# Block 2's keys and queries turned by TensorE inside block 1's units

## The chip, the cores and the metric

The kernel runs on one core of one Trainium2 chip. The metric is the device time of one execution in microseconds (us); lower is better. Before the change the median of 7 runs is 243.35 us (242.52 to 245.54).

## What is computed

Chunked attention with a few memory keys, and then a gated feed-forward layer on its output. Inputs and the output are float32.

```python
# q, k, v: (4, 8, 768, 64); mem_k, mem_v: (4, 8, 8, 64)
for c in range(24):                               # chunks of 32 queries
    l_start, r_end = max(0, 32*c - 16), min(768, 32*c + 32 + 8)
    k_full = concat([mem_k, k[:, :, l_start:r_end]], axis=2)
    v_full = concat([mem_v, v[:, :, l_start:r_end]], axis=2)
    scores = q[:, :, 32*c:32*c + 32] @ k_full.T / 8
    out[:, :, 32*c:32*c + 32] = softmax(scores) @ v_full
x = out.transpose(0, 2, 1, 3).reshape(3072, 512)
y = (maximum(x @ w_gate, 0) * (x @ w_val)) @ w_out    # 512 -> 1536 -> 512
```

## The kernel before

The 3072 rows of x are cut into 8 blocks of 384 tokens (half a sequence each; `TB`, `NB`). For each block the attention is done for four pairs of heads (`hp` 0 to 3). A block has four groups of 96 queries (three chunks each), and each group sees 8 memory rows and a band of 120 keys, so its scores are a 128 x 96 tile with the keys on the partitions. For scores on TensorE (PE), keys and queries must stand with the head's 64 numbers on the partitions, while in memory they stand by token. The step that brings them there is called a turn here.

There are two kinds of turn. Blocks 0 and 1 load keys and queries in long rows, four tokens (1 KB in float32) to a row (`load_rows`), and TensorE turns them: `turn_pe` issues 8 small matmuls against a 0/1 matrix `sels` that also picks the overlapping windows of the keys, and 8 against the identity for the queries. VectorE (DVE) copies the result from PSUM to `kq` (`turn_copy`): for block 0 in one copy of 896 columns, for block 1 in two of 512 and 384. Blocks 2 to 7 load bands and tokens, one token (256 bytes) to a row (`load_band`, `load_q_tokens`), and `turn_dma` turns them with two DMA transposes that SyncE (SP) issues. From block 4 on, GpSimd (POOL) then copies the queries to a tile with zeros between the two heads of a pair (`spread_q`, `qbds`), with which four wide matmuls make the scores of a pair in place of eight narrow ones (`step_s`).

After the scores ScalarE (ACT) takes the exponential. Blocks 0 and 1 get the sums by a matmul with ones (`wide_d`), their inverse by ScalarE (`wide_e`) and the weighted values by `wide_v`. Later blocks hold ones beside the values in `vwins`, so that one matmul gives values and sums (`step_v`), then come the inverse (`step_e`) and the multiply by VectorE (`step_m`). The 0/1 words of `vwins` are written by `one_words`, memsets on VectorE.

The feed-forward part of a block is 12 units and 3 output units. A unit (`ffn_unit`) is 4 matmuls for the gate and 4 for the value, a ReLU by ScalarE (`gr`) and a product by VectorE (`gv`, L343). An output unit (`out_unit`) is 12 matmuls, a copy by ScalarE, and the store.

The order of the instructions on each engine is written out by hand, and each engine runs its own in that order. Block 0's attention comes first, then block 0's units 2 to 11 with block 1's attention between them. Then `run` walks a list of units and places the four steps of the next block's attention: the scores of pair `hp` after unit `at[hp]`, values and inverse `wait` units later, the multiply one unit after that. The first `run` goes over block 1's twelve units and then the six output units of blocks 0 and 1, with block 2's attention at units 11, 12, 14 and 15. Each later `run` goes over one block's units with the next block's attention.

GpSimd issues all loads from HBM that convert float32 to float16, one after the other; a load waits until the eighth before it has landed. The weights of the units come in column groups (`load_w`): 0 to 256, 256 to 512, 512 to 768, 768 to 1024 and 1024 to 1536. Block 1's rows are loaded after the third of these. PSUM has one tile of two banks for scores (`sps`, tag sc), one bank each for `xo` and `xs`, and four banks for units (`fps`); block 0's turns use two tiles of their own before those four exist.

Of the kernel before, what the change touches and what calls it, by code (L numbers as in the profile page):

```python
# [17 lines left out]
def kernel(  # L18
# [158 lines left out]
    def turn_pe(n, hp):  # L177

        if n == 0:
            ps = pools["t"].tile([128, 2, 512], F32, tag="t", name="kq_ps")  # L180
            kps, qps = ps[:, 0], ps[:, 1, 0:TB]
        else:
            ps, kps, qps = None, bank("k_ps"), bank("q_ps")[:, 0:TB]
        turns[n, hp] = ps, kps, qps
        rk, rq = (t.rearrange("p h (j d) -> p h j d", j=J) for t in rows_of(n))
        sel = sels[n].rearrange("p i t -> p (i t)")
        for j in range(J):
# [10 lines left out]
    def turn_copy(n, hp):  # L198
# [5 lines left out]
        ps, kps, qps = turns.pop((n, hp))  # L204
        if n == 0:
            dve_copy(turns[n][:, hp], ps.rearrange("p a c -> p (a c)")[:, 0:512 + TB])
        else:
            dve_copy(turns[n][:, hp, 0:512], kps)
            dve_copy(turns[n][:, hp, 512:], qps)
# [40 lines left out]
    def step_s(n, hp):  # L250
        sc = sps.tile([128, 2, 512], F32, tag="sc", name="sc_ps")
        view = sc[:, :, 0:TB].rearrange("p a (c m) -> p a c m", m=QB)
        if n < 4:
            score_mms(n, hp, sc, True)
# [120 lines left out]
    def fill(count):  # L375
        for i in range(count):
            nc.tensor.matmul(xo, lhsT=filler[:, 0:128], rhs=filler[:, 0:TB], start=True, stop=True)
# [58 lines left out]
    fetch_mem(memk, mem_k)  # L436
    for c0 in (0, 256, 512):
        load_w(c0, c0 + 256)

# [16 lines left out]
    with tc.tile_pool(name="tps", bufs=2, space=bass.MemoryType.PSUM) as pools["t"]:  # L456
# [9 lines left out]
        turn_copy(0, 1)  # L466
        turn_pe(0, 2)
        turn_copy(0, 2)
        wide_d(0, 0)
        wide_e(0, 0)  # L470
        step_s0(0, 1)
        turn_pe(0, 3)
        turn_copy(0, 3)
    pools["f"] = ctx.enter_context(tc.tile_pool(name="fps", bufs=4, space=bass.MemoryType.PSUM))
    step_s0(0, 2)
    wide_d(0, 1)
    wide_e(0, 1)
    fill(2)
    step_s0(0, 3)
    fill(1)  # L480
    wide_v(0, 0)
# [10 lines left out]
    select(bias, 0.0, -NMEM, [[0, 3]], 1, ALU.is_ge)  # L492
    select(bias, NEG, NMEM + 55, [[32, 3]], -1, ALU.is_ge)
    load_w(768, 1024)

# [13 lines left out]
    load_mem_v(1)  # L509
    load_w(1024, 1536)  # L510

    ffn_unit(0, 2, spare=True)
    zero(words(k16s[0][0:32, 0].rearrange("p h d -> p (h d)")), 0)
    zero(words(k16s[1][96:128, NQ - 1].rearrange("p h d -> p (h d)")), 0)
    load_mem_k(2)
    load_mem_k(3)
    load_band(2, k, k16s)
    load_q_tokens(2)
    turn_dma(2)
    wo_src = moe_w_out.rearrange("(c p) f -> p c f", p=128)  # L520
    for a in range(0, NDC, 4):
        pool_dma(wo[:, a:a + 4, :], wo_src[:, a:a + 4, :])

    def value(n, hp):
        wide_v(n, hp)

# [3 lines left out]

    for m in range(3, 6):
        ffn_unit(0, m)
    one_words(0, 0, 128, 0, NQ, ONE)
    one_words(0, 0, NMEM + 16, 0, 1, 0)
    one_words(0, 0, NMEM, 0, 1, ONE)
    load_band(2, v, vwins)
    load_mem_v(2)
    turn_pe(1, 0)
# [4 lines left out]
    turn_pe(1, 2)  # L543
    turn_copy(1, 2)
    step_s(1, 1)
    turn_pe(1, 3)
    turn_copy(1, 3)
    ffn_unit(0, 6)
    sums(1, 0)
    step_s(1, 2)  # L550
    ffn_unit(0, 7)
    sums(1, 1)
    step_s(1, 3)
    value(1, 0)
    ffn_unit(0, 8)
    value(1, 1)
    sums(1, 2)
    ffn_unit(0, 9)
    value(1, 2)
    sums(1, 3)  # L560
    ffn_unit(0, 10)
    value(1, 3)
    ffn_unit(0, 11)


# [16 lines left out]

    def run(order, n, at, wait, turn_at):
        for u, (b, x) in enumerate(order):
            if n < NB:
                pieces(n, [("m", hp) for hp in range(HP) if u == at[hp] + wait + 1])
                now = [hp for hp in range(HP) if u == at[hp] + wait]
                inner, outer = ("ve", "") if x >= NDC else ("v", "e")
                unit(b, x, [lambda w=(w, hp): pieces(n, [w]) for hp in now for w in inner])
                pieces(n, [(w, hp) for hp in now for w in outer])  # L590
                pieces(n, [("s", hp) for hp in range(HP) if u == at[hp]])
            else:
                unit(b, x)
            if u == turn_at and n + 1 < NB:
                turn_dma(n + 1)
                if n + 1 > 3:
                    spread_q(n + 1)
            if n == 2 and u < len(clear):
                clear[u]()

    def loads(n):
        if n < NB:
            load_band(n, k, k16s)
            if n > 3:
                load_mem_k(n)
            load_q_tokens(n)
            load_band(n, v, vwins)
            load_mem_v(n)

    loads(3)  # L610
    run([(1, m) for m in range(NDC)] + [(b, NDC + t) for b in range(2) for t in range(NT)],
        2, (11, 12, 14, 15), 2, 13)
    pieces(2, [("m", 3)])
    for n in range(2, NB):
        loads(n + 2)
        run([(n, u) for u in range(NDC + NT)], n + 1, (3, 6, 8, 11) if n == 2 else (0, 3, 6, 9), 2, 9)

# [29 lines left out]
```

## Time and profile before

| | before |
|---|---|
| median of 7 runs | 243.35 us |
| time given for the profiled execution | 243.35 us |
| its span in the profile | 241.4 us |
| mean granted TensorE clock | 0.992 |
| TensorE (PE) busy | 228.2 us (95%), 1691 matmuls |
| ScalarE (ACT) busy | 144.0 us (60%) |
| VectorE (DVE) busy | 101.3 us (42%) |
| GpSimd (POOL) busy | 99.3 us (41%) |
| DMA queue of GpSimd | 86896 packets, 15.17 MB |
| DMA queue of SyncE | 24922 packets, 6.43 MB |

The profile is one execution as the hardware profiler recorded it. Its span runs from the program's first instruction to its last, and the time of a run has some more around it. Busy time is a union of instruction times, so an engine that is busy for 95% may still not be at its peak. "Granted clock" is the share of full speed that TensorE was given. A line such as `PE L336 MATMUL g_ps<-xT,wg` names the engine, the line of the kernel, the operation, and the tiles that it writes and reads; an arrow in brackets names what ended the idle time before it.

### The profile page before, as it was taken

The page shows a single profiled execution, that of the slowest core. Times are in us where ns is not written, and L with a number is a line of the kernel's source. Part 1 is how long each engine was busy: PE and PEld are TensorE (multiplying, and loading weights), DVE is VectorE, ACT ScalarE, POOL GpSimd, SP SyncE. Part 2 cuts the span into 40 slices and gives each one's busy share as a digit, 9 for nine tenths or more (in the row PEclk, how much of TensorE's full clock was granted, in tenths as well). Part 3 has the DMA queues.
Part 4 walks back from the last instruction along what each step waited for, and adds up shares of the span by engine and source line. Part 5 has one row for each costly group of instructions (what it writes and reads, how often), then busy time and mean ns, then how long its engine had stood idle before and what let it go on. Part 6 is the DMA issues. An engine that isn't in the chain of part 4 may idle for free.

```text
span 241.4 us, 4514 instructions
## 1 busy us (share of the span) xinstructions
PE 228.2 (95%) x1691; PEld 131.8 (55%) x1691; DVE 101.3 (42%) x199; ACT 144.0 (60%) x300; POOL 99.3 (41%) x124
## 2 busy tenths in 40 slices
PE   7889699999799799999999999999999999999993
PEld 3645565565344356546665566546664666556541
DVE  4536745684011335522564054603652156314400
ACT  3564169434388657965995479727883599533321
POOL 7987775912793140299039800991040000000000
PEclk9999979999999999999999999999999999999999
DMA  7999999999999999959999999499901200020012
GB/s 164 154 172 194 185 195 158 191 166 123 149 164 157 159 210 137 92 71 190 157 106 61 195 127 141 27 163 173 155 3 43 87 0 3 33 97 3 1 43 87
DMA packets 115711, 28.57 MB, mean 118 GB/s; under 512 B 102410, under 2 KB 112618, under 8 KB 115690
## 3 DMA queue, kind: packets, MB, share of 16 engines
q0 software_dynamic: 86896, 15.17, 80.9%
q1 hardware_dynamic: 24922, 6.43, 24.4%
q10 hardware_dynamic: 3872, 6.69, 8.6%
q8 instruction: 13, 0.21, 0.4%
q14 instruction: 8, 0.07, 0.1%
HBM read 31.15 MB, written 6.29 MB: 155 GB/s over the span
## 4 chain that ended last, share of the span: by engine, by line
PE 66%; DMA 16%; POOL 6%; ACT 5%; issue 2%; DVE 1%; SPq 1%; ACTq 0%; POOLq 0%
PE o_ps L361 22%; PE v_ps L336 19%; PE g_ps L336 19%; DMA wv<-in_moe_w_val_dram 8%; DMA qT<-q16n 5%; DMA wo<-in_moe_w_out_dram 3%; POOL vwin L136 3%; PE sc_ps L260 2%; PE xs_ps L300 2%; PE xo_ps L300 2%; ACT rinv L309 2%; DVE xT L315 1%; ACT ex L266 1%; ACT ln L304 1%; POOL wg L166 1%
## 5 line engine op out<-in xcount | busy, mean ns | idle before, releaser
L343 DVE TENSOR_TENSOR gv<-v_ps,gr 128x384 f16<-128x384 f32 x95 | 52.6, 555 | 87.2 <-ACT gr L342 65.0
L336 PE MATMUL g_ps<-xT,wg 128*128 128x384 f16 x380 | 78.5, 326 | 1.3 <-DVE xT L315 1.3
L336 PE MATMUL v_ps<-xT,wv 128*128 128x384 f16 x380 | 78.2, 326 | 0.2 <-DMA wv<-in_moe_w_val_dram 0.2
L361 PE MATMUL o_ps<-wo,gv 128*128 128x512 f16 x288 | 64.7, 379 | 0.0
L342 ACT ACTIVATE gr<-g_ps 128x384 f16<-128x384 f32 x95 | 46.3, 489 | 28.5 <-PE g_ps L336 15.2
L336 PEld LDWEIGHTS <-wv 128*128 128x128 f16 x384 | 36.5, 98 | 24.2 <-issue 1.7
L336 PEld LDWEIGHTS <-wg 128*128 128x128 f16 x384 | 36.6, 98 | 23.0
L361 PEld LDWEIGHTS <-gv 128*128 128x128 f16 x288 | 27.5, 98 | 31.5
L266 ACT ACTIVATE ex<-sc_ps,bias 128x256 f16<-128x256 f32 x84 | 33.4, 470 | 9.3 <-PE sc_ps L235 7.5
L364 ACT COPY o_sb<-o_ps 128x512 f32<-128x512 f32 x24 | 14.1, 587 | 32.6 <-PE o_ps L361 25.6
L136 POOL DMA_DIRECT2D vwin<-in_v_dram x32 | 29.0, 930 | 10.0 <-DMA k<-in_k_dram 3.9
L223 POOL COPY qbd<-qT 64x1536 f16<-64x1536 f16 x8 | 11.7, 1462 | 46.6 <-DMA qT<-q16n 46.4
L315 DVE TENSOR_TENSOR xT<-xo_ps,rinv 64x384 f16<-64x384 f32 x24 | 13.2, 549 | 27.8 <-ACT rinv L309 27.8
L136 POOL DMA_DIRECT2D k<-in_k_dram x24 | 21.5, 905 | 7.2 <-DVE qbd L568 2.8
L162 POOL DMA_DIRECT2D q16n<-in_q_dram x24 | 18.7, 797 | 11.6 <-DMA vwin<-in_v_dram 6.9
L309 ACT ACTIVATE rinv<-ln,mln 64x768 f32<-64x768 f32 x24 | 22.3, 928 | 0.2
L304 ACT ACTIVATE ln<-xo_ps 64x384 f32<-64x384 f32 x24 | 11.7, 488 | 13.4 <-PE xs_ps L300 13.4
L300 PEld LDWEIGHTS <-vwin 128*128 128x128 f16 x192 | 10.8, 98 | 5.9 <-DVE xT L315 2.3
L315 DVE TENSOR_TENSOR xT<-xs_ps,rinv 64x384 f16<-64x384 f32 x24 | 13.2, 550 | 0.7
L300 PE MATMUL xo_ps<-ex,vwin 128*128 128x96 f16 x96 | 11.3, 206 | 0.7 <-ACT ex L266 0.3
L300 PE MATMUL xs_ps<-ex,vwin 128*128 128x96 f16 x96 | 11.1, 206 | 0.8 <-DVE xT L315 0.8
L304 ACT ACTIVATE ln<-xs_ps 64x384 f32<-64x384 f32 x24 | 11.4, 477 | 0.0
(72 smaller groups left out, 121.6 us busy)
## 6 DMA issues: line engine op xcount, KB each, us to landing
out_dram<-o_sb ACTq DMA_DIRECT2D x24, 256.0 KB
vwin<-in_v_dram POOLq DMA_DIRECT2D x24, 120.0 KB, 8.7
q16n<-in_q_dram POOLq DMA_DIRECT2D x24, 96.0 KB, 6.1
k<-in_k_dram POOLq DMA_DIRECT2D x18, 120.0 KB, 7.2
wo<-in_moe_w_out_dram POOLq DMA_DIRECT2D x3, 512.0 KB, 10.2
wg<-in_moe_w_gate_dram POOLq DMA_DIRECT2D x4, 256.0 KB, 7.6
wv<-in_moe_w_val_dram POOLq DMA_DIRECT2D x4, 256.0 KB, 8.3
rk<-in_k_dram POOLq DMA_DIRECT2D x3, 224.0 KB, 8.2
```

The lines of the kernel that those rows point to most:

```text
L136: pool_dma(dsts[p][NMEM + m0:NMEM + m1, i, :, 0:D], src)
L162: pool_dma(q16s[n][:, i], src)
L266: nc.scalar.activation(flat[:, :, :, s], view[:, :, :, s], ACT.Exp, scale=SCALE, bias=bias[:, g:g + 1])
L300: nc.tensor.matmul((xo, xs)[hh][:, QB * i:QB * i + QB], lhsT=vw[:, i, 2 * hp + hh, :], rhs=ex[:, hh, i, :], start=True, stop=True)
L304: nc.scalar.activation(ln[:, hh], (xo, xs)[hh][D:128], ACT.Ln, scale=1.0 / 64.0)
L309: nc.scalar.activation(rinv, lns.pop((n, hp)), ACT.Exp, scale=-1.0, bias=mln64[0:D, :])
L315: nc.vector.tensor_tensor(out=x_of(n)[D * hh:D * hh + D, hp, :], in0=(xo, xs)[hh][0:D], in1=rinv[:, hh, :], op=ALU.mult)
L336: nc.tensor.matmul(ps[a], lhsT=(wg, wv)[a][:, f, 128 * m:128 * m + 128], rhs=xTs[n][:, f, :], start=(f == 0), stop=(f == NFC - 1))
L342: nc.scalar.activation(gr, g_ps, ACT.Relu)
L343: nc.vector.tensor_tensor(out=gvs[n][:, m, :], in0=v_ps, in1=gr, op=ALU.mult)
L361: nc.tensor.matmul(o_ps, lhsT=gvs[n][:, m, 128 * t:128 * t + 128], rhs=wo[:, m, :], start=(m == 0), stop=(m == NDC - 1))
L364: nc.scalar.copy(o_sb, o_ps)
```

## The change

Block 2 is loaded in long rows, and TensorE turns it. `turn_pe` and `turn_copy` take block 2 with the score tile `sps` as their PSUM and one copy of 896 columns. In `run`, block 2's pair `hp` is turned after unit `at[hp] - 1`, its scores follow after unit `at[hp]`, and `at` moves from 11, 12, 14, 15 to 2, 5, 8, 11 of block 1's units. `turn_dma` begins with block 3, and block 3 is the first with `spread_q` and the four wide score matmuls.

Block 1's rows are loaded before the third weight group, and the last group of 512 columns is loaded in two. Block 1's turns start after unit 3 instead of unit 5 of block 0, and units stand between them; the sums of a pair come before the next pair's turn. The memsets of `vwins` for block 2 and of two borders of `k16s` move from between units 2 and 6 to behind unit 11; with them in the text, though on other queues, move the load of block 2's band of v and that of `w_out`. Block 3's scores move from units 3, 6, 8, 11 to 0, 3, 6, 9 of block 2's units. At the start, block 0's third turn and the sums of its first two pairs change places with neighbours, and two of the filler matmuls go.

```diff
--- before.py
+++ after.py
@@ -176,14 +176,15 @@
 
     def turn_pe(n, hp):
 
-        if n == 0:
-            ps = pools["t"].tile([128, 2, 512], F32, tag="t", name="kq_ps")
+        if n != 1:
+            pool, tag = (pools["t"], "t") if n == 0 else (sps, "sc")
+            ps = pool.tile([128, 2, 512], F32, tag=tag, name="kq_ps")
             kps, qps = ps[:, 0], ps[:, 1, 0:TB]
         else:
             ps, kps, qps = None, bank("k_ps"), bank("q_ps")[:, 0:TB]
         turns[n, hp] = ps, kps, qps
         rk, rq = (t.rearrange("p h (j d) -> p h j d", j=J) for t in rows_of(n))
-        sel = sels[n].rearrange("p i t -> p (i t)")
+        sel = sels[n % 2].rearrange("p i t -> p (i t)")
         for j in range(J):
             kj = kps.rearrange("p (r j) -> p j r", j=J)[:, j]
             for hh in range(2):
@@ -202,7 +203,7 @@
             qTs[n] = kq[:, :, 512:].rearrange("p a (i m) -> p i a m", i=NQ)
             turns[n] = kq
         ps, kps, qps = turns.pop((n, hp))
-        if n == 0:
+        if n != 1:
             dve_copy(turns[n][:, hp], ps.rearrange("p a c -> p (a c)")[:, 0:512 + TB])
         else:
             dve_copy(turns[n][:, hp, 0:512], kps)
@@ -250,7 +251,7 @@
     def step_s(n, hp):
         sc = sps.tile([128, 2, 512], F32, tag="sc", name="sc_ps")
         view = sc[:, :, 0:TB].rearrange("p a (c m) -> p a c m", m=QB)
-        if n < 4:
+        if n < 3:
             score_mms(n, hp, sc, True)
             ex = epool.tile([128, 2, NQ, QB], F16, tag="ex", name="ex")
             flat, exs[n, hp] = ex, ex
@@ -434,8 +435,8 @@
     load_band(0, v, vwins)
     load_mem_v(0)
     fetch_mem(memk, mem_k)
-    for c0 in (0, 256, 512):
-        load_w(c0, c0 + 256)
+    load_w(0, 256)
+    load_w(256, 512)
 
     def cast(t, hp, eng):
         dst, src, n = rows_of(0)[t], (kst, qst)[t], (KR + 2, QR)[t]
@@ -464,20 +465,19 @@
         step_s0(0, 0)
         turn_pe(0, 1)
         turn_copy(0, 1)
-        turn_pe(0, 2)
-        turn_copy(0, 2)
         wide_d(0, 0)
         wide_e(0, 0)
+        turn_pe(0, 2)
         step_s0(0, 1)
+        turn_copy(0, 2)
         turn_pe(0, 3)
         turn_copy(0, 3)
     pools["f"] = ctx.enter_context(tc.tile_pool(name="fps", bufs=4, space=bass.MemoryType.PSUM))
+    wide_d(0, 1)
     step_s0(0, 2)
-    wide_d(0, 1)
     wide_e(0, 1)
-    fill(2)
+    fill(1)
     step_s0(0, 3)
-    fill(1)
     wide_v(0, 0)
     wide_d(0, 2)
     wide_e(0, 2)
@@ -491,6 +491,7 @@
     select(bias, NEG, -NMEM, [[-32, 3]], 1, ALU.is_ge)
     select(bias, 0.0, -NMEM, [[0, 3]], 1, ALU.is_ge)
     select(bias, NEG, NMEM + 55, [[32, 3]], -1, ALU.is_ge)
+    load_w(512, 768)
     load_w(768, 1024)
 
     ffn_open(0, (0, 1))
@@ -507,34 +508,18 @@
     zero(vwins[1][96:128, NQ - 1, :, 0:D], 0.0)
     load_band(1, v, vwins)
     load_mem_v(1)
-    load_w(1024, 1536)
-
-    ffn_unit(0, 2, spare=True)
-    zero(words(k16s[0][0:32, 0].rearrange("p h d -> p (h d)")), 0)
-    zero(words(k16s[1][96:128, NQ - 1].rearrange("p h d -> p (h d)")), 0)
-    load_mem_k(2)
-    load_mem_k(3)
-    load_band(2, k, k16s)
-    load_q_tokens(2)
-    turn_dma(2)
-    wo_src = moe_w_out.rearrange("(c p) f -> p c f", p=128)
-    for a in range(0, NDC, 4):
-        pool_dma(wo[:, a:a + 4, :], wo_src[:, a:a + 4, :])
-
-    def value(n, hp):
-        wide_v(n, hp)
+    load_w(1024, 1280)
+    load_w(1280, 1536)
+    load_rows_mem(pool_dma, rows_of(2)[0][KR:KR + 2], 2, 0, H)
+    load_rows(2, 0, 4)
+    load_rows(2, 4, 4)
 
     def sums(n, hp):
         wide_d(n, hp)
         wide_e(n, hp)
 
-    for m in range(3, 6):
-        ffn_unit(0, m)
-    one_words(0, 0, 128, 0, NQ, ONE)
-    one_words(0, 0, NMEM + 16, 0, 1, 0)
-    one_words(0, 0, NMEM, 0, 1, ONE)
-    load_band(2, v, vwins)
-    load_mem_v(2)
+    ffn_unit(0, 2, spare=True)
+    ffn_unit(0, 3)
     turn_pe(1, 0)
     turn_copy(1, 0)
     turn_pe(1, 1)
@@ -542,25 +527,37 @@
     step_s(1, 0)
     turn_pe(1, 2)
     turn_copy(1, 2)
+    ffn_unit(0, 4)
     step_s(1, 1)
+    sums(1, 0)
+    ffn_unit(0, 5)
     turn_pe(1, 3)
     turn_copy(1, 3)
+    step_s(1, 2)
+    sums(1, 1)
     ffn_unit(0, 6)
-    sums(1, 0)
-    step_s(1, 2)
+    step_s(1, 3)
     ffn_unit(0, 7)
-    sums(1, 1)
-    step_s(1, 3)
-    value(1, 0)
+    wide_v(1, 0)
+    sums(1, 2)
     ffn_unit(0, 8)
-    value(1, 1)
-    sums(1, 2)
+    wide_v(1, 1)
+    sums(1, 3)
     ffn_unit(0, 9)
-    value(1, 2)
-    sums(1, 3)
+    wide_v(1, 2)
     ffn_unit(0, 10)
-    value(1, 3)
+    wide_v(1, 3)
     ffn_unit(0, 11)
+    one_words(0, 0, 128, 0, NQ, ONE)
+    one_words(0, 0, NMEM + 16, 0, 1, 0)
+    one_words(0, 0, NMEM, 0, 1, ONE)
+    load_band(2, v, vwins)
+    load_mem_v(2)
+    wo_src = moe_w_out.rearrange("(c p) f -> p c f", p=128)
+    for a in range(0, NDC, 4):
+        pool_dma(wo[:, a:a + 4, :], wo_src[:, a:a + 4, :])
+    zero(words(k16s[0][0:32, 0].rearrange("p h d -> p (h d)")), 0)
+    zero(words(k16s[1][96:128, NQ - 1].rearrange("p h d -> p (h d)")), 0)
 
 
     def clear_q(p, hh):
@@ -580,40 +577,40 @@
 
 
 
-    def run(order, n, at, wait, turn_at):
+    def run(order, n, at, turn_at):
         for u, (b, x) in enumerate(order):
+            now = [hp for hp in range(HP) if n < NB and u == at[hp] + 2]
             if n < NB:
-                pieces(n, [("m", hp) for hp in range(HP) if u == at[hp] + wait + 1])
-                now = [hp for hp in range(HP) if u == at[hp] + wait]
-                inner, outer = ("ve", "") if x >= NDC else ("v", "e")
-                unit(b, x, [lambda w=(w, hp): pieces(n, [w]) for hp in now for w in inner])
-                pieces(n, [(w, hp) for hp in now for w in outer])
+                pieces(n, [("m", hp) for hp in range(HP) if u == at[hp] + 3])
+            inner, outer = ("ve", "") if x >= NDC else ("v", "e")
+            unit(b, x, [lambda w=(w, hp): pieces(n, [w]) for hp in now for w in inner])
+            pieces(n, [(w, hp) for hp in now for w in outer])
+            if n < NB:
                 pieces(n, [("s", hp) for hp in range(HP) if u == at[hp]])
-            else:
-                unit(b, x)
+            if n == 2:
+                for hp in range(HP):
+                    if u == at[hp] - 1:
+                        turn_pe(n, hp)
+                        turn_copy(n, hp)
+                if u < len(clear):
+                    clear[u]()
             if u == turn_at and n + 1 < NB:
                 turn_dma(n + 1)
-                if n + 1 > 3:
-                    spread_q(n + 1)
-            if n == 2 and u < len(clear):
-                clear[u]()
+                spread_q(n + 1)
 
     def loads(n):
         if n < NB:
+            load_mem_k(n)
             load_band(n, k, k16s)
-            if n > 3:
-                load_mem_k(n)
             load_q_tokens(n)
             load_band(n, v, vwins)
             load_mem_v(n)
 
     loads(3)
-    run([(1, m) for m in range(NDC)] + [(b, NDC + t) for b in range(2) for t in range(NT)],
-        2, (11, 12, 14, 15), 2, 13)
-    pieces(2, [("m", 3)])
+    run([(1, m) for m in range(NDC)] + [(b, NDC + t) for b in range(2) for t in range(NT)], 2, (2, 5, 8, 11), 13)
     for n in range(2, NB):
         loads(n + 2)
-        run([(n, u) for u in range(NDC + NT)], n + 1, (3, 6, 8, 11) if n == 2 else (0, 3, 6, 9), 2, 9)
+        run([(n, u) for u in range(NDC + NT)], n + 1, (0, 3, 6, 9), 9)
 
 
 # ---- launch: one core; inputs and outputs as the reference has them ----
```

## Prediction

> **What bounds the kernel now.** I read the page's first two parts, then a table of stages, then TensorE's waits and timeline, then the queue of the engine that each wait names.
>
> ```profile
> PE 228.2 (95%) x1691; PEld 131.8 (55%) x1691; DVE 101.3 (42%) x199; ACT 144.0 (60%) x300; POOL 99.3 (41%) x124
> PEclk9999979999999999999999999999999999999999
> ```
>
> TensorE (PE) is busy for 95% of the span, so the time is its work plus its holes. The one slice with a 7 in the clock row says that TensorE lost its clock once, early.
>
> ```profile
> 25.40:29.30 3.90, 2.00 (x41) 1.80 (x40) 3.29 (x7) 0.00 (x1) 2.40 (x4) 1.00 1.70 191
> 29.30:32.70 3.40, 3.40 (x45) 2.92 (x40) 2.14 (x5) 2.36 (x6) 2.54 (x4) 0.50 1.98 173
> 82.00:110.00 28.00, 26.39 (x196) 14.65 (x195) 12.19 (x22) 18.93 (x40) 11.71 (x13) 1.00 1.40 131
> 136.30:162.30 26.00, 26.00 (x181) 15.57 (x180) 11.09 (x20) 18.06 (x39) 13.22 (x15) 1.00 1.36 121
> ```
>
> Columns: stretch, its length, busy time (and count) of PE, PEld, DVE, ACT, POOL, granted clock, DMA. The last row is a whole steady block: 26 us with no hole. The holes lie before 110 us. After a stretch with PE busy 2.00 of 3.90 us, the clock is 0.50 for 3.4 us.
>
> ```profile
> 26.64 0.54 PE L195 MATMUL q_ps<-ident,rq 96*64 96x96 f16 x8
> 29.07 0.36 PE L235 MATMUL sc_ps<-kq 64*128 64x96 f16 x8 [1.90 <-DVE kq L209]
> 32.92 0.34 PE L336 MATMUL g_ps<-xT,wg 128*128 128x384 f16 x1
> 61.74 0.34 PE L235 MATMUL sc_ps<-qT,kT 64*128 64x96 f16 x8 [1.61 <-DMA qT<-q16n]
> 70.15 0.22 PE L300 MATMUL xs_ps<-ex,vwin 128*128 128x96 f16 x1 [0.39 <-DVE xT L315]
> 70.46 1.46 PE L361 MATMUL o_ps<-wo,gv 128*128 128x512 f16 x6
> 83.73 0.32 PE L336 MATMUL g_ps<-xT,wg 128*128 128x384 f16 x1 [1.27 <-DVE xT L315]
> ```
>
> This is TensorE's timeline: start, length, line and operation, and in brackets the idle time before it with its releaser. Each hole has its own releaser. The first is VectorE's (DVE), whose timeline tells why.
>
> ```profile
> 25.63 0.56 DVE L343 TENSOR_TENSOR gv<-v_ps,gr 128x384 f16<-128x384 f32 x1 [0.74 <-PE v_ps L336]
> 26.35 1.67 DVE L446 MEMSET vwin<- 128x1024 uint32 x3 [0.16 <-issue]
> 27.95 0.61 DVE L208 CAST kq<-k_ps 128x512 f16<-128x512 f32 x1
> 28.50 0.53 DVE L209 CAST kq<-q_ps 128x384 f16<-128x384 f32 x1
> ```
>
> Three memsets of vwin stand in VectorE's queue ahead of the casts that the score waits for.
>
> **What goes away.** (1) The first hole. With the memsets out of the way, the casts follow gv of unit 3 directly. Count from V, the start of that unit's v_ps group: gv ends at V+1.48 (24.71 to 26.19), the two casts (0.61 and 0.53, each starting some 0.07 before the one ahead ends) at V+2.49, TensorE follows 0.05 later; its two turns end at V+2.24. 0.30 us of 1.90 stay (0 to 0.6): -1.60.
> (2) The clock. From 29.07 to 32.92 TensorE does two scores and two turns in 3.85 us. At full clock a turn took 0.75 (25.45 to 26.20) and a score 0.28, with their edges 2.1: -1.75.
> (3) Block 2's DMA transposes, and the hole at 61.74: -1.60.
> (4) In the output units block 2's steps stood two or three units apart with the multiplies in between. From the end of the 12 products that start at 66.64 (12 x 0.216) to 70.46 are 1.23 us, of which 0.34 are eight L300 products; the same again ten microseconds later: -1.8. Afterwards only one pair's value step is left in the output units, and the one before it has been finished for three units.
> (5) The 1.27 us at 83.73: the last multiply now comes three output units earlier.
> (6) From 81.82 to 110.05, block 2's units and outputs took 28.2 us; less (5), 0.9 more than the steady 26.05, in which the scores stand after units 0, 3, 6, 9 instead of 3, 6, 8, 11. The change gives block 3 the steady places: -0.9.
> Sum: -8.9 us.
>
> **What is added.** (7) Four turns of block 2, 16 matmuls each, now within block 1's units: 4 x (0.75 + 0.09 edge) = +3.35; bounds 3.0 and 3.5 without and with edges.
> (8) The memsets have not gone, they have moved. In VectorE's queue gv of unit 11 is now followed by three memsets of vwin (1.83 with gaps) and two of k (0.74 with gaps), gv of block 1's unit 0, a memset of 0.91, gv of unit 1, and then block 2's first cast (L206 row: 1.09 for 896 columns). Count from T, the start of unit 11: gv ends T+2.13, memsets T+4.70, gv T+5.26, memset T+6.32, gv T+6.88, cast T+7.89. TensorE has done units 0 and 1, the turn and unit 2 by T+6.09, and its first score waits for that cast: +1.85. If the gaps are shorter 1.2; longer than 1.9 is not in the rows.
> (9) The other three casts each stand behind the gv of a unit that holds a value step. From the row of such a unit (g_ps 90.13, gv to 93.25) gv ends 3.12 after the unit's start, the cast 4.13; TensorE is at the score after 3.87. +0.3 each, 0.9; bounds 0.6 and 1.5.
> Sum: +6.1. Net -2.8: span 241.4 to 238.6, and with the 1.95 us by which the median of the runs, 243.35, lies over the span, 240.5. That is 1.2% faster; about 1% is what a measurement of this kernel can tell from no change.
>
> **Costed at nothing.** Start-up: the first v_ps product waited at 16.60 for its weights, whose place in the queue is kept; that covers the reordering ahead of it by 0.6 us (bounds -0.2 and +0.3). The queues: GpSimd (POOL) issues five row loads (3.5 us) in place of eight band and token loads (4 x 0.91 + 4 x 0.80 = 6.8), with four times the run length; SP loses two transposes (12.7 us of issue). Block 1's rows pass two weight loads, so they land some 2.7 us earlier (the wg and wv loads of before landed 1.4 us apart), and the third weight group lands when the last rows did, 18.30 + 8.2 (the page's time to landing) = 26.5, for a unit that starts near 25.9 and needs its second half near 26.5. No slack: 0 to 0.7, taken as 0 since only the second half lands last. Block 2's band of v now goes ahead of w_out instead of behind it; they are first read near 49 and 65, and were issued from 42.5 and 39.2 before, behind more. The fifth weight group, now in two parts, landed at 38.1 as one (27.28 + 10.81) for a unit at 37.6; its first part is due near 35 and ends half a load, 2.6 us, sooner. Block 3's scores change from eight L235 products (0.28) to four L260 (0.33), which the steady stage in (6) already holds. They need spread_q for block 3, 2.98 us on POOL, ahead of block 4's loads: hidden while transposes end by 79, worth its lateness if not.
>
> A rule that speaks against the change: the Trainium skill, "TensorE: Matmul & The Clock Gate", section "Part 4: PE-mode transpose", gives about 275 ns for one 128x128 transpose in a kernel's context; 64 at that price would be 17.6 us, and the sum 254.8. The rows decide: sixteen in 0.75 us.
>
> **Rivals.** *The clock falls again* (chance 0.24). For: the hole of (8), 1.85 us, is like the one of 1.90 that was followed by 0.50 for 3.4 us. Against: the hole of 1.61 at 61.74 was not. Price 1.75 as in (2): 242.3. The same time results if the median's executions did not hold (2). The same page, section "Part 1: The HAM clock gate", says that the clock falls after an idle window of about 3.4 us and that the window runs free of the kernel; by that alone neither hole would cost clock, where the trace shows one that did.
> *The third weight group is late behind the rows* (0.11): +0.7, 241.2.
> *Block 3's transposes come late* (0.11), the slower side. Its first score moves to the end of unit 0 of block 2's units, near 82, and now needs kT, qT and the spread. Block 2's pair took from 41.7 to 61.6, 20 us. If block 3's start no earlier than before, at 66.2, and take as long, the spread ends at 89.2 and the score waits 6.9 us: 247.4. It is slower from a spread that ends after 85. Against: block 2's transposes no longer stand ahead, and block 4's took 12.4 us (88.9 to 101.3).
>
> **Numbers.** Main case 0.54; its own range, from all lower and all upper bounds, is 239.0 to 242.0, with four fifths under 240.9. Faster by over 1%: 0.54 x 0.8 = 0.43. Within 1%: the fifth, 0.24 and 0.11, 0.46. Slower by over 1%: 0.11. The range is 239.0 to 243.3.
>
> **What would show it.** Right: no half clock near 29; a first hole of about 0.3 near 24.5; a hole of 1.5 to 1.9 on DVE kq ahead of block 2's first score, near 46, and three of 0.3 behind it; no waits on qT or xT between 60 and 110; block 3's units starting near 107 instead of 110. Wrong: a wait on qbd or kT near 82, on wg or wv near 26 or 35, or a second stretch with the clock at 0.50.

## The result, and the profile after

| | before | after |
|---|---|---|
| median of all executions | 243.8 us (64; 242.01 to 249.71) | 241.16 us (27; 240.35 to 243.7) |
| ratio, 95% interval | | 0.9908 (0.989 to 0.9927) |
| profiled execution: time, span | 243.35, 241.4 us | 240.25, 238.3 us |
| executions with a mean clock of 0.993 or less | 61 of 68 | 3 of 28 |

The kernel became 0.9% faster: 2.6 us in the medians, 3.1 us in the spans of the two profiled executions. A ratio and its interval leave disturbed executions out, a median here does not. The last row counts the executions whose mean clock was recorded (before: those beside e1 to e12; after: the 27 and the profiled one); 0.993 is what 3.4 us at half clock make of a span of this length.

The page after, first TensorE and its neighbours, then the clock by slices:

```profile
PE 228.9 (96%) x1737; PEld 133.5 (56%) x1737; DVE 105.0 (44%) x203; ACT 143.1 (60%) x300; POOL 100.1 (42%) x125
...
PEclk9999999999999999999999999999999999999999
```

TensorE has 46 matmul records and 0.7 us of busy time more, in a span 3.1 us shorter. No slice has lost clock. The same stretches as before, and one that now holds block 2's first score (columns as in the prediction):

```profile
25.40:29.30 3.90, 3.90 (x44) 2.12 (x40) 1.89 (x4) 3.05 (x9) 2.61 (x4) 1.00 1.80 182
29.30:32.70 3.40, 3.40 (x47) 2.12 (x46) 1.62 (x3) 3.10 (x8) 2.55 (x5) 1.00 1.95 175
44.40:60.00 15.60, 14.07 (x137) 8.40 (x136) 13.40 (x23) 9.90 (x22) 8.39 (x10) 1.00 1.86 179
82.00:110.00 28.00, 28.00 (x196) 16.91 (x195) 11.65 (x21) 19.87 (x44) 13.06 (x14) 1.00 1.41 124
```

PE was busy for 2.00 of 3.90 us in the first row before and is busy throughout now; the second ran at 0.50 and runs at 1.00; the last was busy for 26.39 us. The third row has 1.53 us of idle time, which is new. TensorE's timeline shows where it lies ("..." marks lines left out, here and below):

```profile
24.63 0.35 PE L236 MATMUL sc_ps<-kq 64*128 64x96 f16 x8 [0.15 <-DVE kq L210]
...
42.73 0.81 PE L337 MATMUL v_ps<-xT,wv 128*128 128x384 f16 x4
43.48 0.63 PE L191 MATMUL kq_ps<-sel,rk 114*64 114x128 f16 x8
43.89 0.54 PE L196 MATMUL kq_ps<-ident,rq 96*64 96x96 f16 x8
44.37 0.82 PE L337 MATMUL g_ps<-xT,wg 128*128 128x384 f16 x4
...
47.21 0.34 PE L236 MATMUL sc_ps<-kq 64*128 64x96 f16 x8 [1.37 <-DVE kq L207]
...
52.08 0.81 PE L337 MATMUL v_ps<-xT,wv 128*128 128x384 f16 x4
52.97 0.34 PE L236 MATMUL sc_ps<-kq 64*128 64x96 f16 x8
...
64.77 1.47 PE L362 MATMUL o_ps<-wo,gv 128*128 128x512 f16 x6
...
80.66 0.81 PE L337 MATMUL g_ps<-xT,wg 128*128 128x384 f16 x4
...
106.71 0.81 PE L337 MATMUL g_ps<-xT,wg 128*128 128x384 f16 x4
```

Of the first hole 0.15 us is left. The score at 47.21 is block 2's first, and it waits for a cast (L207). The lines at 64.77, 80.66 and 106.71 are the first output unit, block 2's first unit and block 3's first unit; between 64.77 and 106.71 no wait on qT or xT is left. VectorE's timeline has the reason for the 1.37 us:

```profile
41.77 1.67 DVE L447 MEMSET vwin<- 128x1024 uint32 x3 [0.16 <-issue]
43.45 0.27 DVE L559 MEMSET k<- 32x256 uint32 x1
...
44.83 0.91 DVE L447 MEMSET vwin<- 128x1024 uint32 x1 [0.16 <-issue]
45.66 0.49 DVE L344 TENSOR_TENSOR gv<-v_ps,gr 128x384 f16<-128x384 f32 x1
46.07 1.08 DVE L207 CAST kq<-kq_ps 128x896 f16<-128x896 f32 x1
```

The first line holds the three memsets of the hole at 29 us before. They have moved to another place ahead of a cast, and now the two on k (before at 22.73 and 23.11) and the long one of 0.91 us (before at 46.65) stand in the same queue.

By stages, from the starts of the lines named:

| stage | before | after | difference |
|---|---|---|---|
| start to block 0's unit 2 (gv_ps) | 20.16 | 20.06 | -0.10 |
| units of blocks 0 and 1, to the first output unit | 41.86 | 44.71 | +2.85 |
| output units, to block 2's first unit | 19.80 | 15.89 | -3.91 |
| block 2, to block 3's first unit | 28.23 | 26.05 | -2.18 |
| the rest | 131.35 | 131.59 | +0.24 |

### The profile page after: what moved, and what is told of

It is laid out like the page before. It is cut to its first block, busy times and chain, and to the rows that moved or that the text cites. A ratio compares the mean times of both kernels' runs of the same rounds, so it can differ in the third digit from the quotient of the medians.

```text
span 238.3 us, 4598 instructions
## 1 busy us (share of the span) xinstructions
PE 228.9 (96%) x1737; PEld 133.5 (56%) x1737; DVE 105.0 (44%) x203; ACT 143.1 (60%) x300; POOL 100.1 (42%) x125
## 4 chain that ended last, share of the span: by engine, by line
PE 86%; DVE 5%; DMA 2%; ACT 2%; issue 2%; POOL 1%; DVEq 0%; POOLq 0%
PE o_ps L362 26%; PE g_ps L337 25%; PE v_ps L337 23%; PE sc_ps L261 3%; DMA rk<-in_mem_k_dram 2%; PE xo_ps L301 2%; PE xs_ps L301 2%; DVE kq L207 2%; DVE gv L344 2%; PE sc_ps L236 1%; DVE vwin L447 1%; PE xo_ps L292 1%; ACT ln L305 1%; PE xs_ps L279 1%; ACT gr L343 1%
## 5 line engine op out<-in xcount | busy, mean ns | idle before, releaser
L362 PE MATMUL o_ps<-wo,gv 128*128 128x512 f16 x288 | 63.5, 379 | 0.0
L337 PEld LDWEIGHTS <-wg 128*128 128x128 f16 x384 | 36.0, 98 | 22.7
L362 PEld LDWEIGHTS <-gv 128*128 128x128 f16 x288 | 28.0, 98 | 33.0
L224 POOL COPY qbd<-qT 64x1536 f16<-64x1536 f16 x10 | 14.6, 1462 | 60.7 <-DMA qT<-q16n 60.4
L136 POOL DMA_DIRECT2D k<-in_k_dram x20 | 17.9, 904 | 0.4 <-issue 0.4
L162 POOL DMA_DIRECT2D q16n<-in_q_dram x20 | 15.6, 802 | 5.0 <-DMA wo<-in_moe_w_out_dram 5.0
```

What stands on the lines that cost most here:

```text
L136: pool_dma(dsts[p][NMEM + m0:NMEM + m1, i, :, 0:D], src)
L162: pool_dma(q16s[n][:, i], src)
L224: nc.gpsimd.tensor_copy(qbds[n % 2][s, :, :, hh, :].rearrange("p i a m -> p (i a) m"), qTs[n][s].rearrange("p i a m -> p (i a) m"))
L337: nc.tensor.matmul(ps[a], lhsT=(wg, wv)[a][:, f, 128 * m:128 * m + 128], rhs=xTs[n][:, f, :], start=(f == 0), stop=(f == NFC - 1))
L362: nc.tensor.matmul(o_ps, lhsT=gvs[n][:, m, 128 * t:128 * t + 128], rhs=wo[:, m, :], start=(m == 0), stop=(m == NDC - 1))
```

## The experiments

Every experiment ran beside the kernel before on the same chip, and its ratio is to that kernel. "The changed kernel" is the kernel after. The main theory is the prediction's: TensorE's work and holes add up, so a hole that goes is worth its length, and a hole that comes costs it. The first four runs were to show the parts.

**e1: the moved memsets, early.**

```diff
     ffn_unit(0, 4)
+    one_words(0, 0, 128, 0, NQ, ONE)
+    one_words(0, 0, NMEM + 16, 0, 1, 0)
+    one_words(0, 0, NMEM, 0, 1, ONE)
     step_s(1, 1)
...
     turn_copy(1, 3)
+    one_words(1, 0, 128, 0, NQ, ONE)
...
     ffn_unit(0, 7)
+    zero(words(k16s[0][0:32, 0].rearrange("p h d -> p (h d)")), 0)
+    zero(words(k16s[1][96:128, NQ - 1].rearrange("p h d -> p (h d)")), 0)
...
-    clear = [lambda: one_words(1, 0, 128, 0, NQ, ONE),
+    clear = [lambda: None,
```

> The changed kernel with its memsets moved: the three for block 2's vwin behind unit 4 of block 0, the long one for block 3's behind block 1's last turn, the two borders of k behind unit 7, all at places where VectorE's timeline shows it idle for 0.9 to 2.3 us. Theory (the hole of 1.37 us ahead of block 2's first score is these memsets in VectorE's queue): the hole shrinks to under 0.3, the span from 238.3 to about 237.0, the time by 1.3 us to near 239.9. Rival (the score waits for its cast of 1.08 us anyway, and VectorE only fills a wait with the memsets): over 1.0 us of the hole stays, 241.

Measured: 241.02 us, 0.988 (0.9832 to 0.9929); span 238.8. The hole ahead of block 2's first score is gone, and yet the time is that of the changed kernel. TensorE's timeline shows two new waits in its place:

```profile
27.65 0.82 PE L337 MATMUL v_ps<-xT,wv 128*128 128x384 f16 x4 [0.65 <-DMA wv<-in_moe_w_val_dram]
...
37.56 0.36 PE L292 MATMUL xo_ps<-ex,vwin 128*64 128x96 f16 x8 [0.71 <-DVE xT L294]
```

The second comes from the edit. VectorE's timeline has the two k memsets at 36.28 and 36.64, ahead of the xT that releases `xo`; behind unit 7 the queue had no room for them. The first is the third weight group, whose wv landed at 27.60 us (26.06 in the changed kernel's profile). From the changed kernel's 238.3: less 1.37, plus 0.38 for a later start (gv_ps at 20.44), 0.65 and 0.71 is 238.67.

**e2: block 1's part alone.** The changed kernel, but block 2 is loaded by tokens and turned by DMA transposes, and its attention stands at the places of before. It keeps block 1's order, the order of the weight loads and the split fifth group; block 3's places, the two memsets on k and the load of `w_out` are those of before.

```diff
-        if n != 1:
+        if n == 0:
...
-    load_rows_mem(pool_dma, rows_of(2)[0][KR:KR + 2], 2, 0, H)
-    load_rows(2, 0, 4)
-    load_rows(2, 4, 4)
...
+    load_mem_k(2)
+    load_mem_k(3)
+    load_band(2, k, k16s)
+    load_q_tokens(2)
+    turn_dma(2)
...
-    run([(1, m) for m in range(NDC)] + [(b, NDC + t) for b in range(2) for t in range(NT)], 2, (2, 5, 8, 11), 13)
+    run([(1, m) for m in range(NDC)] + [(b, NDC + t) for b in range(2) for t in range(NT)],
+        2, (11, 12, 14, 15), 2, 13)
...
```

> Only the part on block 1: its rows ahead of the third weight group, its turns between units, no memsets in front of its casts. Block 2 is loaded by token, turned by DMA and placed as before. Theory (terms 1 and 2, the first hole and the clock that it costs, carry the gain, while block 2's turn gives about as much as it costs): no hole over 0.3 near 24, no half clock, but the wait on qT near 57 and the waits on xT stay; about 3 us under before, 240.5, level with the whole change. Rival (block 2's turn carries the gain): about 1 us under before, 242.5.

Measured: 245.87 us, 1.0085 (1.0052 to 1.0119), slower than before. Both the theory (240.5) and its rival (242.5) fell here. TensorE's timeline around block 2's first score:

```profile
56.44 0.81 PE L337 MATMUL v_ps<-xT,wv 128*128 128x384 f16 x4
61.26 0.51 PE L236 MATMUL sc_ps<-qT,kT 64*128 64x96 f16 x8 [4.01 <-DMA qT<-q16n]
61.70 5.30 PE L362 MATMUL o_ps<-wo,gv 128*128 128x512 f16 x12
```

Block 1's last unit starts its v_ps at 56.44, where before it was 59.31: 2.9 us were won. But the score comes at 61.26, where before it was 61.74. The first transpose was issued at 41.29 here and at 41.72 before, when the last band of k had landed (41.24 and 41.51), and the pair took 20 us in both. The wait on qT takes back what was won ahead of it. It costs more than that, since here the clock fell to 0.50 at the end of the hole and stayed there (windows around it):

```profile
57.25:61.25 4.00, 0.00 (x1) 0.02 (x1) 0.56 (x1) 0.00 (x0) 1.68 (x3) 0.91 1.91 153
61.25:67.35 6.10, 6.09 (x28) 2.24 (x28) 0.00 (x0) 1.52 (x4) 5.04 (x7) 0.50 2.36 150
```

Twelve output products took 5.30 us at a clock of 0.50, 2.76 before.

**e3: block 2's part alone.** The kernel before, with block 2's rows, turns and places and block 3's places as in the changed kernel; block 1's order, the memsets and the weight loads stay.

```diff
-        if n == 0:
+        if n != 1:
...
-    load_mem_k(2)
-    load_mem_k(3)
-    load_band(2, k, k16s)
-    load_q_tokens(2)
-    turn_dma(2)
+    load_rows_mem(pool_dma, rows_of(2)[0][KR:KR + 2], 2, 0, H)
+    load_rows(2, 0, 4)
+    load_rows(2, 4, 4)
...
-        2, (11, 12, 14, 15), 2, 13)
-    pieces(2, [("m", 3)])
+    run([(1, m) for m in range(NDC)] + [(b, NDC + t) for b in range(2) for t in range(NT)], 2, (2, 5, 8, 11), 13)
...
```

> Only the part on block 2: long rows, turned by TensorE in block 1's units, block 3 with the wide scores and the steady places. Block 1's rows, turns and memsets stand as before. Theory: the first hole of 1.9 us and the clock at 0.50 behind it stay; gained are 1.6 + 1.8 + 1.3 + 0.9 = 5.6 from the later holes, paid are 3.35 for the turns, 0.5 for three late casts and some 0.4 for the one long memset left in front of the first cast: 1.3 us under before, near 242. Rival: all of the change's 2.6 us.

Measured: 244.37 us, 1.0019 (0.999 to 1.0049): no gain. The qT wait is gone, the hole of 1.90 us at 28.85 is still there, and a new wait follows (TensorE's timeline):

```profile
38.62 1.46 PE L337 MATMUL v_ps<-xT,wv 128*128 128x384 f16 x4 [1.38 <-DMA wv<-in_moe_w_val_dram]
```

The stretches behind the two holes, by windows:

```profile
29.10:32.00 2.90, 2.44 (x47) 1.98 (x43) 2.36 (x5) 2.27 (x6) 1.54 (x3) 1.00 2.17 165
...
38.60:42.00 3.40, 3.38 (x20) 1.52 (x21) 1.02 (x2) 1.05 (x2) 2.96 (x4) 0.50 1.41 201
```

In this execution the clock held behind the hole of 1.90 us, so TensorE came to the fifth weight group earlier than before and met its wv before it had landed (38.57; in the kernel before 38.09, for a v_ps that started at 38.29). The clock fell there instead. Behind the first output unit e3 has the stages of the changed kernel (15.89 us to block 2's first unit, 26.05 to block 3's), 6.1 us less than before. Ahead of it, from gv_ps to the first output unit, it takes 49.36 us, where the kernel before takes 41.86 and the changed kernel 44.71. So the later gains are all there, and the part on block 2 pays for them in units that still hold the first hole and meet the fifth weight group.

**e4: e1, and block 2's turns one unit further ahead of their scores.**

```diff
-                    if u == at[hp] - 1:
+                    if u == at[hp] - 2:
```

> The kernel with the memsets moved, and each turn of block 2 one unit earlier (behind unit at - 2, so two units stand between a turn and its scores). Theory: the three scores that wait 0.16 each for their cast no longer wait, another 0.4 to 0.5 us, near 239.4. Rival: turn and scores share one tile of PSUM, so the turn now waits for the exponentials of the pair before it, and nothing is gained or up to 1 us lost.

Measured: 240.63 us, 0.9854 (0.9805 to 0.9903), not to be told from e1 by the intervals. The 0.71 us wait on xT is there again (0.72).

After these four, a second theory stood beside the first: before the change, two landings set a floor under TensorE's progress, the fifth weight group at 38 us and block 2's transposes at 61 to 62 us. What is won ahead of a floor is waited for at the floor. The chain of work that ended last, as the profile of the kernel before infers it, speaks for this:

```profile
27.28 10.81 DMA wv<-in_moe_w_val_dram
38.09 0.28 issue
38.38 0.77 POOL q16n L162
39.15 0.07 issue
39.22 7.46 DMA wo<-in_moe_w_out_dram
46.67 2.36 SPq L214
49.03 0.05 issue
49.22 12.38 DMA qT<-q16n
61.60 0.14 issue
61.74 0.34 PE sc_ps L235 x8
```

The lines give start, length and what it was. From 27.28 to 61.74 the chain holds no piece of TensorE; in this stretch it runs through GpSimd's queue of loads and the transposes. The next runs were to tell the two theories apart and to finish e1.

**e5: e4, with the two k memsets where VectorE has room.** One stands behind unit 10 and one behind unit 11.

```diff
     ffn_unit(0, 7)
-    zero(words(k16s[0][0:32, 0].rearrange("p h d -> p (h d)")), 0)
-    zero(words(k16s[1][96:128, NQ - 1].rearrange("p h d -> p (h d)")), 0)
...
     ffn_unit(0, 10)
+    zero(words(k16s[0][0:32, 0].rearrange("p h d -> p (h d)")), 0)
     wide_v(1, 3)
     ffn_unit(0, 11)
+    zero(words(k16s[1][96:128, NQ - 1].rearrange("p h d -> p (h d)")), 0)
```

> The memsets of v's ones early among block 0's units and block 2's turns one unit further ahead of their scores, as in e4, and the two k memsets no longer behind unit 7 but one behind unit 10 and one behind unit 11. Theory (VectorE's queue is what the memsets cost, and it has gaps of 0.7 us between the gv of units 10 and 11): the 1.37 us hole ahead of block 2's first score is gone, the 0.71 us wait on xT that e1 and e4 showed near 37.5 us is gone too, and the three late casts of 0.16 us are gone: span 236.5 to 237.0, time 238.6 to 239.2. Rival (the landing of the third and fifth weight groups sets the pace of block 0's units, so what is won ahead of it is waited for there): waits on wv grow, 240.4 to 241.0.

Measured: 239.44 us, 0.9818 (0.9768 to 0.9868), span 237.3. This beats the changed kernel, whose interval begins at 0.989. TensorE's timeline:

```profile
27.08 0.82 PE L337 MATMUL v_ps<-xT,wv 128*128 128x384 f16 x4 [0.44 <-DMA wv<-in_moe_w_val_dram]
...
46.39 0.34 PE L236 MATMUL sc_ps<-kq 64*128 64x96 f16 x8
```

Block 2's first score has no wait any more, and the wait on xT is gone. The third weight group holds TensorE back by 0.44 us. 238.3 less 1.37 plus 0.44 is 237.4, so the earlier turns add next to nothing: the second score comes 5.61 us behind the first, and the others still come 5.75 us apart, 5.76 in the changed kernel. The lateness of 0.15 us that stood ahead of them stands ahead of the turns now.

**e6: the fifth weight group in one load**, as before the change, at its place in the changed kernel.

```diff
-    load_w(1024, 1280)
-    load_w(1280, 1536)
+    load_w(1024, 1536)
```

> The changed kernel with the fifth weight group in one load each for wg and wv (columns 1024 to 1536), at the same place in the queue. Theory (the weights land just ahead of their use): in the changed kernel the first half of that group's wv landed at 34.70 us and its unit's v_ps began at 34.83; as one load it lands when the second half did, near 37.4, so TensorE waits 2.5 us on wv: 243.7, and 245.4 if the clock falls behind that hole. Rival (the split is worth nothing): 241.2.

Measured: 244.19 us, 0.9984 (0.9941 to 1.0027). No gain is left that can be told from none. TensorE's timeline:

```profile
35.47 0.82 PE L337 MATMUL g_ps<-xT,wg 128*128 128x384 f16 x4 [0.52 <-DMA wg<-in_moe_w_gate_dram]
38.07 0.82 PE L337 MATMUL v_ps<-xT,wv 128*128 128x384 f16 x4 [1.78 <-DMA wv<-in_moe_w_val_dram]
```

The two waits make 2.30 us; the span, 241.5, is 3.2 us longer than that of the changed kernel, of which 0.72 lie ahead of them in a later start (gv_ps at 20.78 instead of 20.06). Five of its ten executions had a mean clock of 0.993 or less.

**e7: the kernel before without its first hole.**

```diff
-    one_words(0, 0, 128, 0, NQ, ONE)
-    one_words(0, 0, NMEM + 16, 0, 1, 0)
-    one_words(0, 0, NMEM, 0, 1, ONE)
-    load_band(2, v, vwins)
-    load_mem_v(2)
     turn_pe(1, 0)
...
     ffn_unit(0, 6)
+    one_words(0, 0, 128, 0, NQ, ONE)
+    one_words(0, 0, NMEM + 16, 0, 1, 0)
+    one_words(0, 0, NMEM, 0, 1, ONE)
+    load_band(2, v, vwins)
+    load_mem_v(2)
```

> The kernel before, with the three memsets of vwin (and the loads that follow them) moved from ahead of block 1's first turn to behind the unit that follows its fourth turn; nothing else. The 1.90 us hole at 29 us and the half clock behind it should be gone, 3.35 us of TensorE's time. Additive theory (each hole is worth its length): 240.0 to 240.5. Floor theory (before, TensorE's progress is set by landings: wv of the fifth group at 38.1 us, for a unit whose v_ps began at 38.29, and block 2's transposes that end near 61.6): a new wait of about 3 us on wv near 35 us and the same wait on qT, block 2's first score again at 61.5 to 62: 243.0 to 244.0, or up to 245.5 if the clock falls behind one of the two waits.

The loads of block 2's band of v move along with the memsets. Measured: 244.03 us, 1.000 (0.9964 to 1.0037). A hole of 1.90 us went and the time did not move. The profiled execution was one of its longest, so its lines (TensorE's timeline) are read only for what TensorE waited on:

```profile
38.63 0.82 PE L336 MATMUL v_ps<-xT,wv 128*128 128x384 f16 x4 [1.72 <-DMA wv<-in_moe_w_val_dram]
...
62.80 0.35 PE L235 MATMUL sc_ps<-qT,kT 64*128 64x96 f16 x8 [2.32 <-DMA qT<-q16n]
```

Both floors show. The additive theory, 240.0 to 240.5, is out for this edit.

**e8: block 1's rows behind the third weight group again.**

```diff
     load_w(256, 512)
+    load_w(512, 768)
...
-    load_w(512, 768)
     load_w(768, 1024)
```

> The changed kernel with block 1's rows behind the third weight group again, as the kernel before had them. Theory: each of the two weight loads takes 1.36 us, so the rows land 2.7 us later (first heads' rq near 23.9 instead of 21.2, the others' near 26.0 instead of 23.3); block 1's first turn, which began at 22.75, waits on rk and rq for 0.8 to 1.0 us and the third turn for 0.2 or less; unit 4's weights land before they are needed: 242.0, and 243.8 if the clock falls. Rival (the order of these loads is worth nothing): 241.2.

Measured: 241.79 us, 0.9896 (0.9844 to 0.9947). The time lies near the theory's 242.0, 0.6 us above the changed kernel, but the ratio lies slightly below the changed kernel's 0.9908, and the intervals overlap. The profile cannot show the wait: in that execution TensorE was slow to start (gv_ps at 21.62), so the rows were in time (it shows no wait on rk or rq). What this order is worth stays open, between nothing and about a microsecond.

**e9: block 3's old places.**

```diff
-        run([(n, u) for u in range(NDC + NT)], n + 1, (0, 3, 6, 9), 9)
+        run([(n, u) for u in range(NDC + NT)], n + 1, (3, 6, 8, 11) if n == 2 else (0, 3, 6, 9), 9)
```

> The changed kernel with block 3's scores again behind units 3, 6, 8 and 11 of block 2 instead of 0, 3, 6 and 9. Step (6) of the prediction says that the places are worth 0.9 us: block 2's stage (from its first unit to block 3's first) grows from 26.05 to 26.9 or 27.0 us, span near 239.2, time 242.0. Rival (the 0.9 us came from block 3's other form of scores or from the DMA transposes, not from the places): 241.2.

Measured: 241.83 us, 0.9949 (0.9915 to 0.9984). The time lies between theory and rival, and the interval overlaps the changed kernel's, so the stage has to decide. Block 2's stage by TensorE's timeline:

```profile
81.19 0.81 PE L337 MATMUL g_ps<-xT,wg 128*128 128x384 f16 x4
...
97.07 0.20 PE L301 MATMUL xo_ps<-ex,vwin 128*128 128x96 f16 x1 [0.40 <-ACT ex L267]
...
107.84 0.81 PE L337 MATMUL g_ps<-xT,wg 128*128 128x384 f16 x4
```

It took 26.65 us, 0.60 more than in the changed kernel. The shown 0.40 us is the value step of the pair whose score stood only two units behind the one before it: its exponential was not done. So the places are worth two thirds of the 0.9 us; where the rest lies is not shown.

**e10: the old order of block 0's start.**

```diff
+        turn_pe(0, 2)
+        turn_copy(0, 2)
         wide_d(0, 0)
         wide_e(0, 0)
-        turn_pe(0, 2)
         step_s0(0, 1)
-        turn_copy(0, 2)
...
-    wide_d(0, 1)
     step_s0(0, 2)
+    wide_d(0, 1)
     wide_e(0, 1)
-    fill(1)
+    fill(2)
     step_s0(0, 3)
+    fill(1)
```

> The changed kernel with block 0's start in the order of before: the third turn ahead of the first pair's sums, the sums of the second pair behind the third score, and three filler products instead of one. The prediction costed this part at nothing, -0.2 to +0.3: the first g_ps, which began at 16.33 us in the changed kernel, begins between 16.0 and 16.4, behind it the weights set the pace: 240.9 to 241.5. Rival (the order of the start is worth half a microsecond or more, as in the summaries of before, 16.01, and after, 16.33, only that the weights hid it): 240.6 or 241.8.

Measured: 240.89 us, 0.9914 (0.9882 to 0.9946). Nothing, as costed: the first v_ps then waits 0.43 us for wv at 16.65.

**e11: a wider hole.**

```diff
-    clear = [lambda: one_words(1, 0, 128, 0, NQ, ONE),
+    clear = [lambda: [one_words(1, 0, 128, 0, NQ, ONE) for _ in range(2)],
```

> The changed kernel with the memset of 0.91 us that stands ahead of block 2's first cast done twice: the hole ahead of block 2's first score grows from 1.37 by 0.91 and a gap of 0.16 to 2.44 us. Theory (length decides: before, a hole of 1.90 us was followed by the clock at 0.50 for 3.4 us): the clock falls, 1.07 + 1.75 us, 244.0. Rival (the clock doesn't follow from one hole's length: holes of 1.90 and 1.78 us in e3 and e6 were followed by full clock, one of 1.38 in e3 by half): 1.07 us alone in most executions, 242.2.

Measured: 244.0 us, 1.0031 (0.9988 to 1.0074). The hole is 2.56 us long in the profile, where the clock held:

```profile
48.80 0.34 PE L236 MATMUL sc_ps<-kq 64*128 64x96 f16 x8 [2.56 <-DVE kq L207]
```

The line is from TensorE's timeline. Of six executions, two had a mean clock of 0.997 or more and took 241.67 and 241.91; four had 0.984 to 0.993 and took 243.79 to 245.15. Both theories are half right: length does not decide one execution, but the longer hole cost clock in more of them, four of six against 3 of 28 in the changed kernel.

**e12: e7, with the fifth weight group split.**

```diff
-    load_w(1024, 1536)
+    load_w(1024, 1280)
+    load_w(1280, 1536)
```

> As e7 (the kernel before with the three memsets moved, so the hole at 29 us is gone), and the fifth weight group split into two loads each for wg and wv, in the order of before. Floor theory: the first half of that group now lands near 36 instead of 38.6 us, so the wait of 1.7 us on wv that e7 showed shrinks to a few tenths, and the wait on qT ahead of block 2's first score grows by the same, to 3.5 to 4 us, since block 2's transposes still end near 61.5: 243.5 to 244.5, or up to 246 where the clock falls behind that hole. Additive theory (a wait taken away is worth its length): 1.5 us less than e7, 242.5 or below.

Measured: 246.33 us (four executions), 1.0139 (1.0056 to 1.0222). No wait on wv is left in the profile, and the wait on qT is longer than in e7 (TensorE's timeline):

```profile
61.15 0.34 PE L235 MATMUL sc_ps<-qT,kT 64*128 64x96 f16 x8 [3.80 <-DMA qT<-q16n]
```

A hole was taken from the kernel before and a load was made to land earlier, and it became slower. All four executions lost clock (0.979 to 0.993). The four kernels with DMA transposes for block 2 have its first score at 61.74, 61.26, 62.80 and 61.15 us, whatever was won ahead.

## Why the prediction was right, and where it was not

The time, 241.16, lies in the range and 0.66 above the 240.5 of the prediction; the ratio, 0.9908, is just inside 1%, where the main case had 1.2%. The main case happened in the profiled execution: its signs are there, though the hole ahead of block 2's first score, 1.37 us, is shorter than the 1.5 to 1.9 named, and of the rivals neither the late transposes of block 3 nor a second stretch at half clock.

- Steps (1), (2) and (3), the holes at 29 and 61 us and the clock: all gone. As a sum they were right, since all three went together. As single terms they were not: e7 took away (1) and won nothing, and e12, which also made the fifth group land earlier, lost. Nor was (2) worth its 1.75 us by itself: the seven executions of the kernel before that kept their clock (0.997 or more) took 242.08 to 244.12 us, median 243.06, and the 33 with 0.99 to 0.993, about one stretch of 3.4 us at half clock, wherever it lay, had a median of 243.4. The reason is that before the change TensorE was not simply bound by its own work. It met the fifth weight group at 38 us with 0.2 us to spare, and the transposes with 1.6 us to wait. The prediction gave landing times for both and did not say that they were floors.
- The fifth group "in two parts" was costed at nothing, and the gain rests on it: as one load it makes TensorE wait 2.30 us (e6); by the ratios this is 1.9 us of time, by the medians 3.0. The prediction had its first part due near 35 and 2.6 us sooner than the 38.1 of before; that is 35.5. By its own figures this is too late, since (1) and (2) bring the v_ps that started at 38.29 to 34.94. It landed at 34.70 for a v_ps at 34.83. That it was in time, by 0.13 us, is luck as far as the prediction goes.
- Step (4), 1.8: the output units took 3.91 us less, of which three scores (3 x 0.28) and three value steps (3 x 0.34) had moved ahead. 2.05 remain.
- Steps (5) and (6), 1.27 and 0.9: together 2.18, as forecast. Of (6) the places alone make 0.60 (e9); what makes the other 0.3 is open.
- Step (7), 3.35: mis-sized. From the start of a turn to what follows it are 0.89 us (43.48 to 44.37), and the v_ps ahead of it takes 0.75 up to the turn (42.73 to 43.48) instead of the 0.65 up to another unit. The first turn lengthens the stage by 0.99 and the others by 0.98 each, 3.93 in all, above the upper bound of 3.5: a turn has an edge on either side, and one was counted.
- Step (8), 1.85: 1.37. VectorE's queue ran 0.2 us faster than counted (the cast ended 7.68 behind T = 39.47, not 7.89), and TensorE was free 0.28 later (T + 6.37, not 6.09): 0.15 of this lies at the two edges of the turn, most of the rest in the end of the last group, which takes 0.81 us where a group with another behind it takes 0.65. e1 and e5 confirm the mechanism: with the memsets elsewhere the hole is gone.
- Step (9), 0.3 each: 0.15 each, 0.89 us instead of 0.74 from the start of v_ps to the score (52.08 to 52.97). The cast ends as counted, 4.12 us behind the start of its unit at 48.79; TensorE comes 0.16 later than counted, again by the edges of the turn.
- The stage of (1) to (3) and (7) to (9) was forecast at +1.15, and at +3.01 with the three scores and three value steps that moved into it. It came to +2.85. Cheaper than forecast were (8) by 0.48, (9) by 0.45 and (1) by 0.15; dearer were (7) by 0.58 and the clock by 0.24 (two turns and two scores take 2.34 us, not 2.1). The errors cancel to -0.26, so that the sum is better than its terms; 0.10 is not assigned.
- The rival of the late third weight group (0.11) is not in the profile after, but five of the nine profiled kernels with its order of loads show it, with 0.30 to 0.65 us. It would fit the 0.66 by which the median lies above the forecast: the profiled execution after was the fastest of its 28, the median of their spans is 239.05 against its 238.3, and the distance of time from span is as counted (median 1.96). That this wait is what makes the other spans longer is argued, not shown, since they have no timeline.
- The rival of the falling clock (0.24): in 3 of 28 executions.

On the clock, the Trainium skill, "TensorE: Matmul & The Clock Gate", section "Part 1: The HAM clock gate", says that the clock falls after an idle window of about 3.4 us and that the window runs free of the kernel. e2's hole of 4.01 us agrees. The holes of 1.90 (before) and 1.38 us (e3), each followed by 0.50 for 3.4 us, do not. That the same length of 1.90 us cost clock in the profile of the kernel before and not in e3's would fit a free-running window; no run here shows the window itself.

## What to carry to other kernels

Before adding up the holes of a busy engine, list the times at which it meets data that only just landed: each is a floor, and a gain ahead of a floor is worth nothing until the floor moves. So an edit that pays may be two that are each worthless or harmful alone, and a load split in two can be what the gain rests on. When work is moved out of a queue's way, move it to a place where the trace shows that queue idle for as long as the work takes, not merely to another place.

## What the runs showed of the hardware

A hole does not cost clock by its length alone: in the profiles, holes of 1.38 us (e3) and 1.90 us (before) were followed by a clock of 0.50, and holes of 1.90 us (e3) and 2.56 us (e11) were not. Executions with a mean clock of 0.993 or less, by the longest waits of TensorE that the kernel's profile shows between 20 and 65 us:

| longest waits | executions with less clock |
|---|---|
| 0.44 us (e5) | 0 of 6 |
| 0.71 and 0.72 us (e1, e4) | 3 of 12 |
| 1.36 or 1.37 us (after, e8, e9, e10) | 7 of 46 |
| 1.78 us (e6) | 5 of 10 |
| 1.90 and 1.38 us (e3) | 9 of 12 |
| 1.90 and 1.61 us (before) | 61 of 68 |
| 1.72 and 2.32 us (e7) | 8 of 12 |
| 2.56 us (e11) | 4 of 6 |
| 3.80 us (e12) | 4 of 4 |
| 4.01 us (e2) | 12 of 12 |

The share grows with the waits, though not in every row, and single executions differ both ways; the waits are those of one profiled execution of each kernel. In some executions the clock was lost at the start, ahead of these waits (from 16.8 to 20.2 us in e4's and e8's profiles), and that is counted here too.
